# Tiles 6 and 7 transposed by DMA, weights loaded in halves and behind transposes, and a new order, in a two-block linear-attention kernel

## The chip, the cores and the metric

One Trainium2 chip, one core. The metric is device time in microseconds (us) of one execution; the profile is of one such execution and is shown in us from the start of its span. Names of engines: PE is the matrix engine (PEld its weight loads), ACT the scalar engine, DVE the vector engine, POOL the GpSimd engine, SP the engine that issues the DMAs.

## What is computed

Four layers, attention (A), dense (B), A, B, on one sequence of 2048 rows of 512 bf16 numbers; each is added to its input.

```python
x = A_x
x = x + _A_ref(_layernorm(x), A_wqkv, A_wo)
x = x + _B_ref(_layernorm(x), B_w1, B_w2)
x = x + _A_ref(_layernorm(x), A_wqkv, A_wo)
x = x + _B_ref(_layernorm(x), B_w1, B_w2)
```

A is linear attention with 32 heads of 16: q, k, v are the three 512-wide parts of `x @ wqkv`; with `phi(t) = (t + 1 if t > 0 else exp(t)) + 1e-6`, each head forms `kv = phi(k)^T v` and `z = sum phi(k)`, and the output is `(phi(q) kv) / (phi(q) z + 1e-6)` times `wo`. B is `relu(x @ w1) @ w2` with 1376 hidden columns.

## The kernel before, in words

The 2048 rows are 16 tiles of 128 rows; four tiles make a chunk (tile i is in chunk i // 4). All weights and activations stay on the chip. The kernel doesn't write its instructions down in order: each step is added to a graph with what it reads and writes (`_Graph.add`, `add_flex` for a step that either of two engines may do), and a list scheduler (`_list_schedule`) puts the steps of each engine into one fixed order, by a planner's costs (`C_...`) and a table `HINTS` that moves single steps forward or back or picks an engine (a key with "!"). So a new table moves steps everywhere. Each engine then runs its own order and waits in it for semaphores; nothing overtakes. PSUM has 8 banks of 128 x 512; a step that opens a bank waits until the one before in it was read out.

The start of the first layer, with the names that the planner uses and their lines:

- `ld_x0`, `ld_x1`, `ld_x2`, ... (L465, L471): input tiles 0, 1, 2 to 3, 4 to 7, 8 to 11, 12 to 15. `ld_wk`, `ld_wq`, `ld_wv0` (L470), `ld_wvl` (L479), `ld_wo`, `ld_w1`, `ld_w2a`, `ld_w2b` (L481 to L488): the weights. All DMAs are issued by SP, in one order, on one queue.
- `bnst`, `bnag` (L534, L535, DVE) make mean and variance of a tile. `lnv`, `rstd` make the inverse deviation: for tiles 0 to 3 and for whole chunks 2 and 3 on ACT (L540, L542), for tiles 4 to 7 as `veps` on DVE and a power on POOL (L545, L547). `norm` (L572, DVE) writes the normalized tile to `xn`.
- `trp` (L600, PE) transposes tiles 0 to 7 with four 128-wide matmuls against an identity, `trev` (L606 ACT, L607 DVE) copies the result from PSUM to `Tb`. After `trp` of tiles 0 and 1 there is a `fill` (L529), four matmuls on zeros. Tiles 8 to 15 are transposed by DMA, two tiles at a time (`tr2_0` to `tr3_1`, L586), as are all tiles in the later layers.
- `kproj` (one tile, four matmuls of 512 columns, one for each quarter of the contraction over 512), `qh` (chunk 0, half a chunk, four steps of four 256-column matmuls) and `qproj` (a chunk, four steps) are the products with wk and wq (L635, as are all matmul groups). Each result is read twice by ACT (`lin` L618, `exp` L620), then `em` (L622) and `phi` (L628) on DVE make phi of it.
- `g0_3`, `g0_0`, ... (PE) collect `phi(k)^T` times the normalized tiles; the first ones need phi of the four tiles of chunk 0. They have no read-out on ACT until all chunks are in.

At the end of the first layer `fin` (PE, one tile each) makes the output of a tile, `resid` (L642, DVE) adds it, `sq` (L650, ACT) and small steps on POOL and DVE make the statistics, `norm` (L576 DVE or POOL, L581 ACT) normalizes, and `tr0_0`, `tr0_1`, `tr1_0`, ... (L586) transpose by DMA; `tr1_1` holds tiles 6 and 7. The second layer then begins with `hr0`, `h0_0`, ..., `hr1`, where `hr1` needs the four tiles of chunk 1; `trh0` (L826) is a DMA transpose of the result of `hr0`.

Of the kernel before, what the change touches and what calls it, by code (L numbers as in the profile page):

```python
# [1385 lines left out]
```

## Time and profile before

| what | value |
|---|---|
| median of 3 runs | 268.78 us (268.74 to 269.23) |
| the profiled execution | 268.93 us, of which the span of its instructions is 267.2 us |
| PE busy, instructions | 262.0 us, 2020 matmuls recorded |
| DVE, ACT, POOL busy | 226.2, 187.0, 58.5 us |
| granted clock of PE | full in every slice |
| HBM read, written | 7.14 MB, 2.10 MB |

The page lists groups of instructions by line, engine and tiles (`out<-in`). The chain of waits follows the end of the span back from each instruction to what released it. The view of waits adds up the idle time of an engine by what ended it. The view of one tile gives, for instructions that touch it, durations, starts and, for DMAs, the time from issue to landing. The timeline merges equal instructions that follow each other ("x4"); the length of a merged row of matmuls holds the latency of its last one too, the chain's does not.

### The profile page before, as it was taken

To read this page: it belongs to the slowest core of one execution; us is meant where nothing else is said; L and a number is where in the kernel's file an instruction comes from. 1 tells how busy PE (TensorE), PEld (TensorE's weight loads), DVE (VectorE), ACT (ScalarE), POOL (GpSimd) and SP (SyncE) were. 2 spreads that over 40 slices of the span, in tenths; PEclk is the share of its full clock that TensorE was granted. 3 is DMA by queue.
4 is the path that set the end of the run, shared out by engine and by line. 5 is a ranking of instruction groups with operands and counts; after the bars stand their busy time and mean duration, and the time that the engine had idled before them with its cause. 6 is when DMAs were issued, how large, how long until landed. Compare 5 with 4: busy or idle time off the path is not lost.

```text
span 267.2 us, 5481 instructions
## 1 busy us (share of the span) xinstructions
PE 262.0 (98%) x2020; PEld 183.1 (69%) x2020; DVE 226.2 (85%) x636; ACT 187.0 (70%) x408; POOL 58.5 (22%) x146
## 2 busy tenths in 40 slices
PE   7999999999989999999999999999999999999995
PEld 3664547644745798857768755674488789888884
DVE  5799974789888999997998675459999999899994
ACT  4998896766975237999667797787899936057400
POOL 3210000026682001403103430000744434000000
PEclk9999999999999999999999999999999999999999
DMA  7986620763765000400400421054373223402003
GB/s 205 368 285 137 197 42 3 157 146 65 86 120 98 2 20 2 89 11 2 79 2 0 79 54 28 2 129 108 62 153 68 39 39 101 81 0 72 28 34 126
DMA packets 44890, 22.18 MB, mean 83 GB/s; under 512 B 34784, under 2 KB 43328, under 8 KB 44864
## 3 DMA queue, kind: packets, MB, share of 16 engines
q1 hardware_dynamic: 44864, 21.83, 34.3%
q8 instruction: 16, 0.26, 0.4%
q14 instruction: 10, 0.08, 0.1%
HBM read 7.14 MB, written 2.10 MB: 35 GB/s over the span
## 4 chain that ended last, share of the span: by engine, by line
PE 92%; ACT 3%; DMA 3%; DVE 1%; SPq 0%; issue 0%; DVEq 0%
PE ps L635 91%; ACT sqscr L650 2%; DMA Tb<-xn 2%; DMA xin<-in_A_x_dram 1%; PE ps L600 1%; ACT xn L581 1%; DVE xres L642 0%; DVE bst L534 0%; PE ps L529 0%; DVE rdc L1064 0%; SPq L471 0%; DVEq L1324 0%; DVE xn L572 0%; ACT big L946 0%
## 5 line engine op out<-in xcount | busy, mean ns | idle before, releaser
L618 ACT ACTIVATE big<-ps 128x512 bf16<-128x512 f32 x64 | 40.7, 644 | 9.5 <-PE ps L635 9.4
L650 ACT ACTIVATE sqscr<-xres 128x512 bf16<-128x512 f32 x48 | 30.0, 625 | 9.1 <-DVE xres L642 5.1
L635 PE MATMUL ps<-Tb,w 128*128 128x256 f16 (+1 forms) x216 | 35.3, 304 | 0.0
L635 PE MATMUL ps<-w,big 128*128 128x256 bf16 (+1 forms) x256 | 32.4, 272 | 0.0
L635 PE MATMUL ps<-wqkv,Tb 128*128 128x512 bf16 x128 | 31.2, 379 | 0.0
L635 PE MATMUL ps<-big,xn 128*128 128x256 bf16 (+1 forms) x224 | 31.1, 288 | 0.0
L635 PE MATMUL ps<-Tb,wqkv 128*128 128x512 f16 (+1 forms) x144 | 30.8, 355 | 0.0
L620 ACT ACTIVATE escr<-ps 128x512 bf16<-128x512 f32 x48 | 29.6, 634 | 1.1 <-PE ps L635 1.1
L635 PE MATMUL ps<-Mf,big 128*128 128x512 bf16 x128 | 29.6, 379 | 0.0
L635 PEld LDWEIGHTS ps<-w,big 128*128 128x128 bf16 (+1 forms) x256 | 24.9, 98 | 3.6 <-ACT big L946 0.3
L635 PEld LDWEIGHTS ps<-big,xn 128*128 128x128 f16 x224 | 21.3, 98 | 8.5 <-issue 0.8
L635 PEld LDWEIGHTS ps<-Tb,w 128*128 128x128 bf16 x216 | 20.6, 98 | 8.8 <-DMA Tb<-xn 0.4
L908 ACT ACTIVATE escr<-ps 128x512 f32<-128x512 f32 (+1 forms) x40 | 20.3, 544 | 8.1 <-PE ps L635 7.4
L895 DVE TENSOR_TENSOR big<-ps,escr 128x512 bf16<-128x512 f32 (+1 forms) x40 | 23.6, 603 | 1.7 <-ACT escr L908 1.1
L564 POOL TENSOR_TENSOR rstd<-veps,nhalf 128x2 f32<-128x2 f32 x24 | 20.4, 853 | 7.9 <-DVE veps L562 6.8
L635 PEld LDWEIGHTS ps<-Tb,wqkv 128*128 128x128 bf16 x144 | 13.7, 98 | 11.7 <-ACT escr L620 0.3
L635 PEld LDWEIGHTS ps<-Mf,big 128*128 128x128 bf16 x128 | 12.3, 98 | 13.8 <-ACT Mf L717 0.2
L622 DVE TENSOR_SCALAR escr<-escr 128x512 bf16<-128x512 bf16 x48 | 13.7, 289 | 8.6 <-ACT escr L620 8.4
L635 PEld LDWEIGHTS ps<-wqkv,Tb 128*128 128x128 f16 x128 | 12.2, 98 | 12.4 <-ACT Tb L606 0.4
L628 DVE TENSOR_TENSOR big<-big,escr 128x512 bf16<-128x512 bf16 x48 | 19.8, 419 | 0.8 <-ACT big L618 0.2
L581 ACT ACTIVATE xn<-xres,nbias,rstd 128x512 f16<-128x512 f32 x21 | 16.8, 815 | 5.1 <-DVE nbias L566 3.9
L898 ACT ACTIVATE big<-big 128x512 bf16<-128x512 bf16 (+1 forms) x31 | 16.2, 542 | 4.8 <-DVE big L895 4.7
(116 smaller groups left out, 515.9 us busy)
## 6 DMA issues: line engine op xcount, KB each, us to landing
big<-rdc SPq DMA_DIRECT2D x32, 128.0 KB, 2.7
wqkv<-in_A_wqkv_dram SPq DMA_DIRECT2D x3, 512.0 KB, 7.0
xin<-in_A_x_dram SPq DMA_DIRECT2D x3, 512.0 KB, 7.8
w<-in_B_w_dram SPq DMA_DIRECT2D x1, 1376.0 KB, 14.5
w<-in_B_w_dram SPq DMA_DIRECT2D x1, 1280.0 KB, 7.0
wo<-in_A_wo_dram SPq DMA_DIRECT2D x1, 512.0 KB, 10.3
out_dram<-GT SPq DMA_DIRECT2D x1, 512.0 KB, 4.1
out_dram<-Mf SPq DMA_DIRECT2D x1, 512.0 KB, 2.6
```

Of the source, the lines that this page charges most:

```text
L564: g.add(POOL, lambda e: e.tensor_tensor(rstd[:, sl], veps[:, sl], nhalf[:, 0:n], ALU.pow), [("veps", lo), ("nhalf",)], [("rstd", i) for i ...
L581: (ACT, lambda e: e.activation(xn[:, i, :], src, ACTF.Identity, scale=rstd[:, i:i + 1], bias=nbias[:, i:i + 1]), C_ACT_SB_AP)],
L600: last = e.transpose(psb()[:, 128 * c:128 * c + 128], xn[:, i, 128 * c:128 * c + 128], ident[:])
L618: g.add(ACT, lambda e: e.activation(dst_ap, psv[:, b, :], ACTF.Identity, bias=1.0 + 1e-6, scale=1.0), [("ps", b)], [dst_key], C_ACT_PSUM, ...
L620: g.add(ACT, lambda e: e.activation(sap, psv[:, b, :], ACTF.Exp), [("ps", b)], skeys, C_ACT_EXP, name=name + "_exp")
L622: g.add(DVE, lambda e: e.tensor_scalar(sap, sap, 1.0, 1e-6, ALU.min, ALU.add), skeys, skeys, C_DVE_BF4X, name=name + "_em")
L628: g.add(DVE, lambda e: e.tensor_tensor(dst_ap, dst_ap, sap, ALU.max), [dst_key] + skeys, [dst_key], 340.0, name=name + "_phi")
L635: last = e.matmul(o, l, r, start=st, stop=sp, skip_group_check=skip)
L650: g.add(ACT, lambda e: e.activation(sqscr[:, q, :], xres[:, i, :], ACTF.Square, scale=math.sqrt(INV_D), accum_out=s2[:, i:i + 1]), xr(i), ...
L895: g.add(DVE, lambda e: e.tensor_tensor(ap, sh(psv[:, bank, 0:w]), sh(other()), ALU.add), [("ps", bank)] + okeys + ([] if first else bk), q ...
L898: g.add_flex([(ACT, lambda e: e.activation(ap, ap, ACTF.Relu), C_ACT_PSUM if len(cs) == 2 else 270.0), (DVE, lambda e: e.tensor_scalar(ap, ...
L908: g.add(ACT, lambda e, w=w: e.activation(q[:, 0:w], psv[:, bank, 0:w], ACTF.Identity), [("ps", bank)], key, C_ACT_PSUM if len(cs) == 2 els ...
```

## The change

- **Tiles 6 and 7**: statistics together on ACT, and one DMA transpose (`tr1_1`) in place of two `trp`; tiles 0 to 5 stay on PE. The rule `hi - lo >= 2` sends that pair's `lnv` and `rstd` to ACT.
- **Loads**: wk and wq come in two halves of the contraction each (`wka`, `wkb`, `wqa`, `wqb`). `wv0` and `wvl` are tied behind the norms of tiles 6 and 7, `wo`, `w1` and `w2` behind those of tiles 12 to 15.
- **First use in halves**: `kproj` of tiles 0 and 1 and the `qh` steps are split by halves of the contraction.
- **Zeros**: the `fill` after tile 1 is gone.
- **First norms** of tiles 1 to 7 may go to POOL; the planner's table put none there.
- **New order**: another `HINTS` table, and other planner values for when loads land.

The order that the scheduler makes of it, at the start, by the planner's names (the first norms are called `fnorm` in the changed kernel and `norm` here; a `kproj` or `qh` with a last digit 0 or 1 is one half of the contraction):

```
SP before  ld_x0 ld_x1 ld_x2 ld_wk ld_x4 ld_wq ld_x12 ld_x8 ld_wv0 ld_wvl ld_wo ld_w1 tr2_0 tr2_1 ld_w2a ld_w2b tr3_1 tr3_0
SP after   ld_x0 ld_x1 ld_wka ld_x2 ld_wkb ld_wqa ld_x4 ld_wqb ld_x12 ld_x8 tr1_1 ld_wvl ld_wv0 tr2_0 tr2_1 tr3_1 tr3_0 ld_wo ld_w1 ld_w2a ld_w2b

PE before  trp0 fill0 trp1 fill1 kproj0 trp2 kproj1 trp3 kproj2 kproj3 qh0_0_3 qh0_1_3 qh0_0_0 qh0_0_1 trp4 ... kproj4 trp5 g0_3_0 g0_0_0
PE after   trp0 fill0 trp1 kproj0_0 kproj0_1 kproj1_0 [qh, first half of wq, x4] kproj1_1 trp2 trp3 [qh, second half, x4]
           kproj2 kproj3 [qh of tiles 2 and 3, x4] trp4 [qh x2] trp5 [qh x2] kproj4 kproj5 qproj1_1 kproj6 kproj7 qproj1_2 qproj1_3 g0_3_0 g0_0_0

DVE after  bnst0 bnag0 bnst1 norm0 bnag1 norm1 bnst2 bnst3 bnag2 bnag3 k0_em norm2 norm3 bnst6 bnst7 bnst4 bnag6 bnag7 bnag4 bnst5
           veps4 k1_em bnag5 norm6 veps5 norm7 norm4 k1_phi norm5 k2_em k3_em k2_phi bnst12 bnst14 bnag12 bnst9 bnag14 k4_em
           bnag9 bnst11 bnst8 bnag11 k0_phi bnag8 bnst10 q0_2_em bnag10 k4_phi q0_2_phi k3_phi

ACT after  lnv0 rstd0 lnv1 rstd1 trev0 trev1 lnv2 k0_exp rstd2 lnv3 rstd3 k1_lin trev2 trev3 k1_exp lnv6 k0_lin rstd6
           k2_lin k2_exp k3_lin k3_exp trev4 q0_0_lin trev5
```

At the end of the first layer `fin7` stands two `fin` steps earlier among the others (before `fin12` and `fin13`, not behind them), the norm of tile 6 is on DVE (behind `resid15`) and no longer on ACT, and on SP `tr1_1` stands ahead of `trh0`.

The core of the diff:

```diff
-        ld_w(slice(D, 2 * D), "wk")
+        ld_w(slice(D, 2 * D), "wka", slice(0, 2))
         ld_x(2, 4)
-        ld_w(slice(0, D), "wq")
+        ld_w(slice(D, 2 * D), "wkb", slice(2, 4))
+        ld_w(slice(0, D), "wqa", slice(0, 2))
+        ld_w(slice(0, D), "wqb", slice(2, 4))
...
+        def tied(load, names):
+            n = len(g.ops)
+            load()
+            for o in g.ops[n:]:
+                o.sdeps += [p for p in g.ops[:n] if p.name in names and p not in o.sdeps]
...
-            if i < 2:
+            if i < 1:
                 warm_fill(i)
...
+            parts = ((0, 1, "wka"), (2, 3, "wkb")) if first_k and i < 2 else ((0, 1, 2, 3, "wka", "wkb"),)
...
+                for k, key in enumerate(("wqa", "wqb")):
+                    mm_group(lambda b=b, j=j, k=k: [(psv[:, b, 256 * h:256 * h + 256], wqkv[:, c, 128 * j:128 * j + 128], Tb[:, i0:i0 + 2, c, :],
+                                                     h == 0 and c == 0, c == 3, True) for c in (2 * k, 2 * k + 1)],
+                             [("T", i0), ("T", i0 + 1), (key,)], [("ps", b)], 2 * C_MM256, "qh%d_%d_%d_%d" % (t, h, j, k))
...
-                if t < FIRST_PE_CHUNKS:
+                if t < FIRST_PE_CHUNKS and i < 6:
...
+            if t == 1:
+                ln_part_first(6, 8)
+                ln_norm(6, True)
+                ln_norm(7, True)
+                tr_dma(1, 1)
...
+            if t == 1:
+                tied(loads_a, ["fnorm6", "fnorm7"])
...
+                        if t + 3 == NCH - 1:
+                            tied(loads_b, ["fnorm%d" % i for i in range(NT - 4, NT)])
```

More of the change, by code (lines that the diff above doesn't have):

```diff
@@ L465, in ld_x, with ld_w @@
             dma(lambda e: e.dma_start(xin[:, lo:hi, :], x_v[:, lo - 1:hi - 1, :]), [], [("xin", i) for i in range(lo, hi)],
-                350.0 * (hi - lo), "ld_x%d" % lo, issue=C_LOAD_ISSUE, late={1: 100.0, 2: 200.0}.get(lo, C_LATE))
+                350.0 * (hi - lo), "ld_x%d" % lo, issue=C_LOAD_ISSUE, late={1: 100.0, 2: 650.0}.get(lo, C_LATE))
         wq_v = A_wqkv.rearrange("(c p) n -> p c n", p=128)
-        def ld_w(sl, key):
-            dma(lambda e: e.dma_start(wqkv[:, :, sl], wq_v[:, :, sl]), [], [(key,)], 1480.0, "ld_" + key, issue=C_LOAD_ISSUE, late=500.0 if key == "wk" else C_LATE)
+        def ld_w(sl, key, cs=slice(0, 4)):
+            dma(lambda e: e.dma_start(wqkv[:, cs, sl], wq_v[:, cs, sl]), [], [(key,)], 370.0 * (cs.stop - cs.start), "ld_" + key,
+                issue=C_LOAD_ISSUE, late=700.0 if key[:2] == "wk" else C_LATE)
@@ L471, in build_kernel @@
         dma(lambda e: e.dma_start(xin[:, 0, :], x_h), [], [("xin", 0)], 370.0, "ld_x0", issue=C_LOAD_ISSUE, late=-350.0)
         ld_x(1, 2)
-        ld_w(slice(D, 2 * D), "wk")
+        ld_w(slice(D, 2 * D), "wka", slice(0, 2))
         ld_x(2, 4)
-        ld_w(slice(0, D), "wq")
+        ld_w(slice(D, 2 * D), "wkb", slice(2, 4))
+        ld_w(slice(0, D), "wqa", slice(0, 2))
+        ld_w(slice(0, D), "wqb", slice(2, 4))
         for t in range(1, NCH):
             ld_x(4 * t, 4 * t + 4)
-        ld_w(slice(2 * D, 3 * D), "wv0")
@@ L487, in build_kernel, with loads_a @@
-        if FLAST < 128:
-            dma(lambda e: e.dma_start(w2[0:FLAST, NFC - 1, :], B_w2[nfull * 128:DFF, :]), [], [("w2b",)], 600.0, "ld_w2b", issue=C_LOAD_ISSUE)
+        def tied(load, names):
[3 more added lines that the diff above has]
+                o.sdeps += [p for p in g.ops[:n] if p.name in names and p not in o.sdeps]
+        def loads_a():
+            ld_w(slice(2 * D, 3 * D), "wv0")
+            dma(lambda e: e.dma_start(wvl[:], A_wqkv[D - 1:D, 2 * D:3 * D].broadcast_to([128, D])), [], [("wvl",)], 2000.0, "ld_wvl",
+                issue=C_LOAD_ISSUE)
@@ new lines, in loads_b @@
+        def loads_b():
+            dma(lambda e: e.dma_start(wo[:], A_wo.rearrange("(c p) n -> p c n", p=128)), [], [("wo",)], 1500.0, "ld_wo", issue=C_LOAD_ISSUE)
+            dma(lambda e: e.dma_start(w1[:], B_w1.rearrange("(c p) n -> p c n", p=128)), [], [("w1",)], 4500.0, "ld_w1", issue=C_LOAD_ISSUE)
+            dma(lambda e: e.dma_start(w2[:, 0:nfull, :], B_w2[0:nfull * 128, :].rearrange("(c p) n -> p c n", p=128)),
+                [], [("w2a",)], 5500.0, "ld_w2a", issue=C_LOAD_ISSUE)
+            if FLAST < 128:
+                dma(lambda e: e.dma_start(w2[0:FLAST, NFC - 1, :], B_w2[nfull * 128:DFF, :]), [], [("w2b",)], 600.0, "ld_w2b", issue=C_LOAD_ISSUE)
@@ L489, in build_kernel @@
         W2KEYS = [("w2a",), ("w2b",)] if FLAST < 128 else [("w2a",)]
-        ALL_LOADS = [("wk",), ("wq",)]
+        ALL_LOADS = [("wka",), ("wkb",), ("wqa",), ("wqb",)]
         def _table(e):
@@ L571, in ln_norm @@
             if first:
-                g.add(DVE, lambda e: e.tensor_scalar(xn[:, i, :], xin[:, i, :], mv[:, i, 0:1], rstd[:, i:i + 1], ALU.subtract, ALU.mult),
-                      [("xin", i), ("mean", i), ("rstd", i)], [("xn", i)], C_DVE_NORM_BF, name="norm%d" % i)
+                f = (lambda e: e.tensor_scalar(xn[:, i, :], xin[:, i, :], mv[:, i, 0:1], rstd[:, i:i + 1], ALU.subtract, ALU.mult))
+                g.add_flex([(DVE, f, C_DVE_NORM_BF)] + ([(POOL, f, C_POOL_NORM)] if 0 < i < 8 else []),
+                           [("xin", i), ("mean", i), ("rstd", i)], [("xn", i)], name="fnorm%d" % i)
                 return
@@ L651, in sq, with a_k @@
                   xr(i), [("sqscr", q), ("s2", i)], C_ACT_SQ, name="sq%d" % i)
-        def a_k(i):
+        def a_k(i, first_k=False):
             b = alloc_bank()
-            mm_group(lambda: [(psv[:, b, :], Tb[:, i, c, :], wqkv[:, c, D:2 * D], c == 0, c == 3, False) for c in range(4)],
-                     [("T", i), ("wk",)], [("ps", b)], 4 * C_MM512, "kproj%d" % i)
+            parts = ((0, 1, "wka"), (2, 3, "wkb")) if first_k and i < 2 else ((0, 1, 2, 3, "wka", "wkb"),)
+            for k, p in enumerate(parts):
+                cs = [c for c in p if isinstance(c, int)]
+                mm_group(lambda cs=cs: [(psv[:, b, :], Tb[:, i, c, :], wqkv[:, c, D:2 * D], c == 0, c == 3, False) for c in cs],
+                         [("T", i)] + [(c,) for c in p if not isinstance(c, int)], [("ps", b)], len(cs) * C_MM512,
+                         "kproj%d" % i if len(parts) == 1 else "kproj%d_%d" % (i, k))
             phi_evac(b, pk_tile(i), ("big", pk_unit(i)), "k%d" % i, stt=(i % 4) < K_STT)
@@ L729, in a_q @@
                                             c == 0, c == 3, False) for c in range(4)],
-                         [("T", i) for i in range(4 * t, 4 * t + 4)] + [("wq",)], [("ps", b)], 4 * C_MM512, "qproj%d_%d" % (t, j))
+                         [("T", i) for i in range(4 * t, 4 * t + 4)] + [("wqa",), ("wqb",)], [("ps", b)], 4 * C_MM512, "qproj%d_%d" % (t, j))
                 q_evac(t, j, b, first)
@@ L740, in a_q_half @@
                 i0 = 4 * t + 2 * h
-                mm_group(lambda b=b, j=j: [(psv[:, b, 256 * h:256 * h + 256], wqkv[:, c, 128 * j:128 * j + 128], Tb[:, i0:i0 + 2, c, :],
-                                            h == 0 and c == 0, c == 3, True) for c in range(4)],
-                         [("T", i0), ("T", i0 + 1), ("wq",)], [("ps", b)], 4 * C_MM256, "qh%d_%d_%d" % (t, h, j))
+                for k, key in enumerate(("wqa", "wqb")):
+                    mm_group(lambda b=b, j=j, k=k: [(psv[:, b, 256 * h:256 * h + 256], wqkv[:, c, 128 * j:128 * j + 128], Tb[:, i0:i0 + 2, c, :],
+                                                     h == 0 and c == 0, c == 3, True) for c in (2 * k, 2 * k + 1)],
+                             [("T", i0), ("T", i0 + 1), (key,)], [("ps", b)], 2 * C_MM256, "qh%d_%d_%d_%d" % (t, h, j, k))
                 if h == 1:
```

12 lines of the change are left out of this document (3 added, 9 removed), and 124 rows, old and new, of the table HINTS.

## Prediction

> **What bounds the kernel now.** I read the page first, its busy times and its chain of what ended last:
>
> ```profile
> PE 262.0 (98%) x2020; PEld 183.1 (69%) x2020; DVE 226.2 (85%) x636; ACT 187.0 (70%) x408; POOL 58.5 (22%) x146
> ...
> PE 92%; ACT 3%; DMA 3%; DVE 1%; SPq 0%; issue 0%; DVEq 0%
> ```
>
> PE works nearly all the time and the chain is PE's: PE sets the end. So an edit is worth what it takes from PE's work, from PE's start or from PE's idle time; all else is cover. Next, PE's own waits. Behind the zeros at the start there is one:
>
> ```profile
> PE ps L635 <- DMA Tb<-xn: 0.8, 1, 0.8
> ```
>
> Third, the chain in order of time (start, us, what):
>
> ```profile
> 6.00 0.56 PE ps L600 x4
> 6.57 0.22 PE ps L529 x4
> 6.79 0.98 PE ps L635 x4
> ...
> 18.37 0.22 PE ps L600 x4
> 18.59 0.87 PE ps L635 x8
> 19.46 0.22 PE ps L600 x4
> 19.69 43.25 PE ps L635 x264
> ...
> 71.85 4.67 DMA Tb<-xn
> 76.51 0.05 issue
> 76.56 187.63 PE ps L635 x1544
> ```
>
> From 6.79 PE is dense; a PE transpose (L600) in the stream costs 0.22 us; at 76.5 PE waits 0.83 for a DMA transpose issued at 71.85 (tiles 6 and 7 of the second layer, ahead of `hr1`); behind it no wait to the end at 264.2. So the whole room is small: 0.22 a transpose, tenths at the start, 0.83.
>
> Last, the landings. The view of the tile wqkv, cut to the issue of wk and then to that of wq, gives
>
> ```profile
> L470 SPq DMA_DIRECT2D wqkv<-in_A_wqkv_dram x1: 434/434/434, 2.2 to 2.2; - x1
> ...
> DMA to landing us min/median/max: 4.5/4.5/4.5
> ```
> ```profile
> L470 SPq DMA_DIRECT2D wqkv<-in_A_wqkv_dram x1: 443/443/443, 3.2 to 3.2; - x1
> ...
> DMA to landing us min/median/max: 7.0/7.0/7.0
> ```
>
> wk lands at 2.2 + 4.5 = 6.7, wq at 3.2 + 7.0 = 10.2. The same view of xin gives tile 0 at 0.8 + 2.1 = 2.9, tile 1 at 1.2 + 2.6 = 3.9, tiles 2 and 3 at 1.7 + 3.1 = 4.8, tiles 4 to 7 at 2.7 + 6.0 = 8.7. Between landings, 256 KB (tiles 2, 3) took 0.9 and 512 KB (wk) 1.9. kproj0 at 6.79 thus followed both wk (6.7) and the end of the zeros (6.57 + 0.22).
>
> **The change, part by part.**
>
> *Two PE transposes gone.* 2 x 0.22 = **-0.44** on PE's stream. Their copies out of PSUM (0.42 each, DVE L607) go too; `veps` and the power on POOL become lnv6 and rstd6 on ACT. That matters only through DVE and ACT below.
>
> *First product earlier.* Without the second zeros PE is free at 6.57. wka stands third in the queue, where 256 KB landed at 4.8; tile 0 is copied out at 5.61 + 0.60 = 6.2. So kproj0 begins at 6.57 and not 6.79: **-0.22**. Its second half needs wkb at 7.0; 1 MB is through by then as before (wk, 6.7). Two bounds: 0 (if the halves come 0.3 late) and -0.3 (PE could not begin before tile 0 is there).
>
> *Second half of wq.* After kproj0 (0.87: four matmuls, by the row 18.59) PE does half of kproj1 (to 7.87; tile 1 is out at 7.2), four half steps of qh (0.87, to 8.74; wqa by about 7.6, a quarter of the way from 6.7 to 10.2), the rest of kproj1 (9.17) and trp2, trp3 (9.61). Then it wants wqb. Ahead of wqb stand the same 2 MB as ahead of the end of wq before, so I take 10.2: PE waits **+0.6**. Nothing hides this: PE's order is fixed, and kproj2 behind it waits too. Bounds: 0 (landing by 9.6) and +1.6 (11.2, under the rivals). Before, PE came to wq only at 10.8, behind kproj2 and kproj3, so this wait is new.
>
> *DVE in front of g0_3.* trp2 and trp3 want norm2 and norm3: k0_exp on ACT starts 0.22 behind kproj0 (6.79 to 7.81 before, less four matmuls), at 7.66, rstd2 0.48 later, rstd3 at 8.5; the norms run at 8.5 and 8.9 and end by 9.3, just in time. Tiles 4 to 7 land at about 9.3 (10.2 less 0.9 for wqb). From 9.3 to the end of k3_phi DVE has, by starts in the timeline, 10 bn_stats of 0.61, 10 bn_aggr of 0.09, 4 norms of 0.32, 5 em of 0.25 (0.21 to 0.29), 6 phi of 0.35 and 2 small ones: 11.6. k3_phi ends at about 21.0. PE, from 10.2, has four half steps of qh (0.9), the eight of tiles 2 and 3 (1.7), kproj2 to 7 (5.2), trp4 and trp5 (0.4) and three qproj (2.6): 10.8, so it comes to g0_3_0 at 21.0. I take **+0.1** (0 to +0.5): before, k3_phi was done by 14.2 and had no part in this.
>
> *Tiles 6 and 7 by DMA.* norm7 ends on DVE about 4.0 after 9.3 (4 bn_stats, 4 bn_aggr, one em, two norms and small ones), so tr1_1 is issued at 13.3, behind nothing on SP that waits longer; tiles 8 to 11, the last load ahead in the queue, land at 4.4 + 8.4 = 12.8. Its own time is 3.0 (the first two of the second layer: 3.0, 3.0) to 5.1 (the one issued at 69.1): landing at 16.3 to 18.4. PE wants it for qproj1_1 at 16.7. I take 3.0, since the queue is empty then as at 62.1, and the wait at **0**. Behind the waiting tr1_1 on SP stand wvl and wv0, not used before 24 (L661).
>
> *Weights behind transposes.* wv0 leaves at about 15, wo to w2 (3.3 MB) with tiles 12 to 15 at about 34. wo is used at 50.2, w1 at 66.2, w2 at 75.5 (L965). At 1 MB in 3.5 us they are in by about 46. Cost 0; the first to feel a delay are the spreads of 1/den, issued from 45.3 on the same queue.
>
> *Order at the end of layer 1.* The 0.83 us stand behind this: norm of tile 6 on ACT, 70.87 + 0.80, then trh0's issue (70.56 + 1.19), then 4.7 of DMA. In the new order fin7 stands two steps (2 x 0.87) earlier, the norm is on DVE behind resid15 (which ended at 70.0), and trh0 stands behind. tr1_1 can leave at about 70.5; even at 4.7 it lands at 75.2, PE comes at 75.7. I take **-0.83**; bounds 0 and -0.83. Elsewhere the order changes too, but PE was dense there: nothing to win, so 0, with what can be lost under the rivals. The stretch behind 264.2 keeps its steps.
>
> Sum: -0.44 - 0.22 + 0.6 + 0.1 - 0.83 = **-0.79**. The profiled execution (268.93, span 267.2) goes to 268.1; it stands 0.15 above the median, so I forecast 268.78 - 0.79 = **268.0 us**.
>
> **The rivals.**
>
> - *No waits at the start*: wqb by 9.6 and k3_phi early. For it: less stands behind the loads. Against: those bytes stood behind before too. -0.44 - 0.22 - 0.83 = -1.49: 267.3.
> - *The wait ahead of hr1 comes back.* For it: those transposes took 5.1 and 4.7, and in 71.5 to 73.9 us the view of the DMAs has a load of code in the same engines:
>
> ```profile
> q8 instruction: 1, 0.02, 4.0%
> ```
>
>   If that hits the earlier tr1_1 harder, or norm6 slips on DVE, only -0.44 + 0.48 = +0.04 is left: 268.8.
> - *Tiles 6 and 7 land late* (the other side). Place: qproj1_1. At 5.1 they land at 18.4 and PE waits 1.7, of which the 0.1 at g0_3 is taken back: -0.79 + 1.6 = +0.8, 269.6. It decides from a landing at about 17.6 on. Against: nothing else is in the queue. The Trainium skill, "VectorE: DVE Perf Modes", Rules for kernel authors, speaks for this rival: transpose 128 x 128 on TensorE where PSUM will do, by DMA only otherwise. By that rule tiles 6 and 7 belonged on PE; the trace agrees on the latency (3.0 against 0.22), not on which of the two is on PE's path.
> - *The halves come slower than wholes.* Tile 1's 128 KB took 1.0 between landings, as much as the 256 KB behind; if each of the two more DMAs costs such a half us, wqb lands at 11.2 and PE loses 0.9 more: +0.1, 268.9. Against: 256 KB in 0.9 and 512 KB in 1.9 are one rate. The Trainium skill, "DMA: Bandwidth & Descriptors", Bandwidth, says to batch DMAs to 1 MiB or more; from its table (64 KB 0.95 us, 1 MB 6.15 us) I estimate 0.7 a split, wqb at 11.6 and 269.3. The 0.9 and 1.9 here don't agree with it.
> - *New waits behind 77 us.* The new order is tight in other places; each wait like the 0.83 costs as much, two of them give +0.87: 269.7. Against: the planner's order of before has one such wait in 260 us.
> - That the change does nothing is out: the built order has 24 PE transposes for 32 and 29 DMA transposes for 28.
>
> **Chances.** Forecast 0.38, no waits at the start 0.18, wait ahead of hr1 0.16, tiles 6 and 7 late 0.10, slow halves 0.06, new waits 0.12. About 0.2% (0.54 us) is what a measurement can tell from no change: below 268.24 counts as faster. Of the forecast's 0.38, 0.26 lies there and 0.12 within (its start terms at their upper bounds): faster 0.26 + 0.18 = 0.44, same 0.12 + 0.16 + 0.06 = 0.34, slower 0.10 + 0.12 = 0.22. The range goes from 267.2 (no waits at the start, PE at tile 0's landing) to 269.6 (tiles 6 and 7 late) and leaves out the new waits and what lies beyond.
>
> **What would show it.** Right: 24 L600 matmuls; the first L635 at 6.5 to 6.6; one PE wait of about 0.6 ending near 10.2, put down to the wqkv load; none at 76. The forecast is wrong if PE has waits behind 22 us, or if the wait for wqb is under 0.2 or over 1.2.

## The result and the profile after

| | before | after |
|---|---|---|
| median of 7 runs each | 268.74 us (268.12 to 269.23) | 270.05 us (269.54 to 271.05) |
| ratio | | 1.0057, 95% interval 1.0035 to 1.0079 |
| the profiled execution, its span | 268.93, 267.2 | 269.73, 267.9 |

The change costs 1.3 us in the median, 0.8 between the two profiled executions; the forecast was 0.8 less. The page of the changed kernel (its lines are some 25 further down in the code, PE's products are L660):

```profile
PE 261.8 (98%) x2008; PEld 182.5 (68%) x2008; DVE 225.7 (84%) x621; ACT 186.5 (70%) x413; POOL 59.5 (22%) x152
...
PE 86%; ACT 6%; DMA 3%; DVE 1%; SPq 1%; issue 1%; POOL 1%; DVEq 0%
```

PE has 12 matmuls fewer and is still the chain, but only for 86% of it instead of 92. PE's waits (us in total, times, longest) name the rest:

```profile
PE ps L660 <- DMA Tb<-xn: 1.1, 1, 1.1
PE ps L660 <- DMA wqkv<-in_A_wqkv_dram: 0.5, 1, 0.5
PE ps L660 <- DVE big L653: 0.2, 1, 0.2
```

and the chain in order of time (start, us, what) says where they are:

```profile
4.19 5.82 DMA wqkv<-in_A_wqkv_dram
10.05 3.65 PE ps L660 x24
...
14.59 149.52 PE ps L660 x1072
...
168.61 0.44 DVE big L653
169.09 14.42 PE ps L660 x112
...
199.24 3.25 DMA Tb<-xn
202.63 62.31 PE ps L660 x580
```

wqb lands at 10.01 and lets PE go on at 10.05, as forecast. The wait at 76 us is gone, as forecast. But at 169 PE waits for phi of tile 13 (`k13_phi`; 0.2 by the view, 0.4 by the records of the matmuls), and at 202.6 for a DMA transpose of tiles 6 and 7, issued at 199.24, this time that of the last layer: a wait that the kernel before does not have.

To see how much each place costs, I took from the records of the matmuls when each kernel has the same PE work left. The table gives that time less the profiled execution of before, at points of before's clock (the experiments' rows are used further down):

| us later than before at | 13 | 57 | 78 | 163 | 188 | 200 | 206 | end |
|---|---|---|---|---|---|---|---|---|
| after | -0.33 | 0.07 | -0.93 | -1.04 | -0.41 | -0.64 | 0.72 | 0.74 |
| g0, after again | 0.56 | 0.96 | -0.04 | -0.16 | 0.47 | 0.24 | 1.63 | 1.65 |
| f1 | 0.16 | 0.67 | -0.33 | -0.45 | 0.17 | 0.15 | 1.76 | 1.78 |
| g1 | 0.44 | 0.88 | -0.12 | -0.24 | 0.39 | 0.17 | 0.93 | 0.95 |
| h1 | 0.30 | 0.87 | -0.13 | -0.26 | 0.37 | 0.77 | 0.77 | 0.79 |
| k1 | 0.04 | 0.51 | -0.49 | -0.62 | -0.03 | -0.25 | 0.34 | 0.36 |
| h3 | -0.32 | 0.46 | -0.54 | -0.67 | -0.45 | 0.62 | 0.62 | 0.64 |
| k2 | -0.33 | 0.45 | -0.55 | -0.67 | -0.45 | -0.06 | -0.06 | -0.04 |
| g5 | 1.11 | 1.51 | 0.51 | 0.37 | 0.37 | 0.95 | 1.25 | 1.31 |
| f4 | 0.31 | 0.31 | 0.23 | 0.12 | 0.12 | 0.07 | 1.00 | 1.07 |
| g6 | -0.24 | -0.24 | -0.23 | 0.64 | 1.27 | 1.04 | 1.66 | 1.67 |
| e6 | 0.41 | 0.63 | 0.66 | 0.55 | 4.80 | 4.80 | 4.80 | 4.81 |
| s1 | 2.45 | 2.45 | 1.84 | 1.80 | 1.80 | 1.76 | 1.76 | 1.80 |

Read the first row by its steps: the start -0.33; to 57 us +0.40 (mostly the `den` steps, below); the wait ahead of `hr1` of the second layer -1.00; to 163 -0.11; the second attention +0.63 (0.4 ahead of `g0_3_3`, 0.2 for a `den`); to 200 -0.23; then +1.36 within 4 us, the wait at 202.6 (1.25 by the starts of PE's products; the view's 1.1 leaves out the latency of the last one) and 0.11 behind it; sum +0.72. The first profile of the changed kernel was also a good one: in g0 it starts 0.9 later, and ends 0.9 later too, so what the start wins or loses is still there at the end. (One execution in the experiments, h2's profiled one, ran at a granted clock of 0.755; it is left out of the ratio, and its trace is not read.)

`den` is a planner's name for four matmuls on 32 columns of the array that make the sums for the divisions. In both profiles a `den` by itself costs 0.2 us more than one that stands next to another; before, five of the eight stood in groups, after only two.

### The profile page after: what moved, and what is told of

Read it like the earlier page. It is cut to its first block, busy times and chain, and to the rows that moved or that the text cites. A ratio compares the mean times of both kernels' runs of the same rounds, so it can differ in the third digit from the quotient of the medians.

```text
span 267.9 us, 5464 instructions
## 1 busy us (share of the span) xinstructions
PE 261.8 (98%) x2008; PEld 182.5 (68%) x2008; DVE 225.7 (84%) x621; ACT 186.5 (70%) x413; POOL 59.5 (22%) x152
## 4 chain that ended last, share of the span: by engine, by line
PE 86%; ACT 6%; DMA 3%; DVE 1%; SPq 1%; issue 1%; POOL 1%; DVEq 0%
PE ps L660 86%; DMA wqkv<-in_A_wqkv_dram 2%; ACT sqscr L675 2%; DMA Tb<-xn 1%; ACT escr L938 1%; DVE xres L667 1%; ACT big L643 1%; ACT escr L645 1%; ACT xn L606 1%; SPq L477 1%; SPq L482 0%; POOL rstd L588 0%; ACT lnd L783 0%; PE ps L625 0%; DVE big L653 0%
## 5 line engine op out<-in xcount | busy, mean ns | idle before, releaser
L643 ACT ACTIVATE big<-ps 128x512 bf16<-128x512 f32 x64 | 39.0, 639 | 10.5 <-PE ps L660 10.5
L660 PE MATMUL ps<-Tb,w 128*128 128x256 f16 (+1 forms) x216 | 36.1, 304 | 0.0
L660 PE MATMUL ps<-w,big 128*128 128x256 bf16 (+1 forms) x256 | 32.3, 272 | 0.0
L660 PE MATMUL ps<-Tb,wqkv 128*128 128x512 f16 (+1 forms) x144 | 31.5, 356 | 0.5 <-DMA wqkv<-in_A_wqkv_dram 0.5
L660 PE MATMUL ps<-big,xn 128*128 128x256 bf16 (+1 forms) x224 | 31.6, 288 | 0.2 <-DVE big L653 0.2
L660 PE MATMUL ps<-wqkv,Tb 128*128 128x512 bf16 x128 | 30.6, 379 | 0.0
L660 PE MATMUL ps<-Mf,big 128*128 128x512 bf16 x128 | 29.4, 379 | 0.0
L660 PEld LDWEIGHTS ps<-big,xn 128*128 128x128 f16 x224 | 21.2, 98 | 9.5 <-issue 0.9
L660 PEld LDWEIGHTS ps<-w,big 128*128 128x128 bf16 (+1 forms) x256 | 24.9, 98 | 3.7 <-ACT big L976 0.3
L660 PEld LDWEIGHTS ps<-Tb,w 128*128 128x128 bf16 x216 | 20.8, 98 | 8.8 <-DMA Tb<-xn 0.2
L660 PEld LDWEIGHTS ps<-Tb,wqkv 128*128 128x128 bf16 x144 | 13.5, 98 | 12.7 <-DMA wqkv<-in_A_wqkv_dram 1.0
L660 PEld LDWEIGHTS ps<-Mf,big 128*128 128x128 bf16 x128 | 12.3, 98 | 13.8 <-DVE Mf L747 0.2
L580 POOL TENSOR_SCALAR mean<-s 128x2 f32<-128x2 f32 x24 | 7.2, 299 | 62.1 <-DVE xres L667 59.6
L660 PEld LDWEIGHTS ps<-wqkv,Tb 128*128 128x128 f16 x128 | 12.5, 99 | 12.4 <-ACT Tb L631 0.5
L588 POOL TENSOR_TENSOR rstd<-veps,nhalf 128x2 f32<-128x2 f32 x24 | 18.8, 784 | 7.1 <-DVE veps L586 6.4
L606 ACT ACTIVATE xn<-xres,nbias,rstd 128x512 f16<-128x512 f32 x19 | 15.2, 810 | 6.6 <-POOL nbias L590 3.4
```

Source lines behind the costliest of these rows:

```text
L580: g.add(POOL, lambda e: e.tensor_scalar(mean[:, sl], s1[:, sl], -INV_D, None, ALU.mult), [("s1", i) for i in tl], [("mean", i) for i in tl ...
L588: g.add(POOL, lambda e: e.tensor_tensor(rstd[:, sl], veps[:, sl], nhalf[:, 0:n], ALU.pow), [("veps", lo), ("nhalf",)], [("rstd", i) for i ...
L606: (ACT, lambda e: e.activation(xn[:, i, :], src, ACTF.Identity, scale=rstd[:, i:i + 1], bias=nbias[:, i:i + 1]), C_ACT_SB_AP)],
L643: g.add(ACT, lambda e: e.activation(dst_ap, psv[:, b, :], ACTF.Identity, bias=1.0 + 1e-6, scale=1.0), [("ps", b)], [dst_key], C_ACT_PSUM, ...
L660: last = e.matmul(o, l, r, start=st, stop=sp, skip_group_check=skip)
```

## The experiments

Each was run beside the kernel before on the same chip, in five batches on five chips (e; f; g; h with s; k). Ratios are to the kernel before of the same batch, with the 95% interval; across batches compare these and not the medians.

| run | median us | ratio |
|---|---|---|
| g0 after again | 270.28 | 1.0064 (1.0039 to 1.0089) |
| e1 | 270.70 | 1.0059 (1.0033 to 1.0085) |
| f1 | 271.29 | 1.0086 (1.0057 to 1.0114) |
| f2 | 271.01 | 1.0078 (1.0049 to 1.0107) |
| f3 | 272.40 | 1.0115 (1.0074 to 1.0156) |
| g1 | 269.82 | 1.0046 (1.0021 to 1.0070) |
| h1 | 269.78 | 1.0033 (1.0010 to 1.0056) |
| h2 | 270.01 | 1.0031 (1.0007 to 1.0055) |
| h3 | 269.26 | 1.0016 (0.9996 to 1.0035) |
| k1 | 269.75 | 1.0044 (1.0019 to 1.0069) |
| k2 | 269.11 | 0.9999 (0.9976 to 1.0022) |
| f4, before with one SP step moved | 269.81 | 1.0031 (1.0006 to 1.0056) |
| s1, before with quarter loads | 270.25 | 1.0042 (1.0017 to 1.0066) |
| e6, before with two den moved | 273.48 | 1.0154 (1.0105 to 1.0203) |
| g5, start after, rest before | 269.28 | 1.0019 (0.9997 to 1.0041) |
| g6, start before, rest after | 270.78 | 1.0072 (1.0047 to 1.0096) |
| e7, e8, mixed hints | 271.53, 291.12 | 1.0092, 1.0798 |

In the orders below a leading digit is the layer, from 0, under which the planner files a step (`2.tr1_1`: made by the second attention, wanted by `3.hr1_0`); lines with + and - are steps moved in the order of one engine.

### First theory: one wait ahead of hr1 (e1, f1, g1)

Theory A: the wait at 202.6 is what the change lost. SP's order in the changed kernel has two issues, `3.trh0` and the spread of 1/den, ahead of the transpose that PE waits for.

```diff
 SP: 2.tr1_0,
+    2.tr1_1,
     3.trh0, 2.spread3_1,
-    2.tr1_1,
     2.spread3_0
```

e1 and f1 have this edit; in e1 the planner also gave out the PSUM banks anew, in f1 everything else is the changed kernel's.

> The changed kernel, with one step moved on SP alone: the DMA transpose of tiles 6 and 7 of the last layer goes ahead of trh0 and of the spread of 1/den that stand in front of it; every other step of every engine keeps its place. Theory A (the new order costs the time: above all the 1.1 us that PE waits at 201.4 for that transpose, issued 199.24, landed 202.49): its inputs are there at 197.0, so it is issued at 197.3, lands by 200.6, PE does not wait, and the time falls by 1.1 to 1.25 us, from 270.05 to about 268.9. Theory B (the edits at the start and the loads cost it, and the wait only shows time that would be lost in any case): the time stays within 0.3 of 270.05.

> The changed kernel again with the DMA transpose of tiles 6 and 7 of the last layer ahead of trh0 and of the spread on SP, and this time with nothing else moved: in the first run of this move (e1) the planner had also given the PSUM banks out anew. Theory A (the wait of 1.25 us ahead of hr1 is what the change lost): -1.1 to -1.25, to about 268.9. Theory C (a wait behind the wait: PE, come 1.2 us earlier, runs into the evictions on ACT that it had been ahead of by nothing, as e1's waits of 0.95 and 0.41 ahead of h5_1_0 and h6_1_0 hint): hr1_0 starts without a wait, but half or more comes back within the next 5 us: 269.4 to 270.1.

Theory A fell. In both `hr1_0` starts without a wait, and nothing is won: between 200 and 206 us f1 loses 1.61 where after lost 1.36. f1's PE waits, the first line:

```profile
PE ps L695 <- DVE big L960: 1.4, 1, 1.4
```

and DVE's timeline behind it (start, us, ..., in brackets idle time before it and what ended it):

```profile
202.89 0.58 DVE L836 TENSOR_TENSOR big<-big 128x512 bf16<-128x512 bf16 x1 [1.59 <-DMA big<-rdc]
```

The spread that was overtaken now lands at 202.87, DVE stands in `pqs3_1` waiting for it, and the read-out that PE needs is queued behind that. g1 serves both: f1, and on DVE

```diff
 DVE: 3.hc22_0_2,
-     2.pqs3_1,
      3.hc22r_0_2, 3.hs1_1, 3.hc11_1_0, 3.hs2_1,
+     2.pqs3_1,
      2.pqs3_0
```

> The changed kernel with the transpose of tiles 6 and 7 of the last layer ahead of trh0 and of the spread on SP, as in f1, and in addition one step moved on DVE: pqs3_1, which waits for that spread, goes four steps back, next to pqs3_0. In f1 DVE waited 1.6 us in pqs3_1 for the spread that now came later, and PE behind it 1.4 for an eviction. Theory A2 (two transfers in a row on SP, each with an early consumer: one wanted by PE, one by DVE; both consumers must be served): no wait ahead of hr1_0 and none ahead of h5_1_0, -1.2 to -1.4 against the changed kernel. Theory C2 (yet another wait follows): less than half of it.

> The changed kernel as it is, once more, beside the other three, as their reference. Expected: about 270 us; and, since in e1 and f1, whose starts are the same, the profiled execution was 0.5 to 0.6 us later at 13 us than in the first profile of the changed kernel, a spread of some 2 us over its executions.

Between 200 and 206 us g1 loses 0.76 where g0 loses 1.39; its median is 0.46 lower. Half: DVE still waits 0.4 for a spread. The reason is seen on SP: five issues stand in a row there from 195 us on, and each of them has a consumer that is early.

### One part of the order alone, in the kernel before (f4)

```diff
 SP: 2.tr1_0, 2.spread3_0, 3.trh0,
+    2.spread3_1,
     2.tr1_1,
-    2.spread3_1,
```

> The kernel before with one part of the new order alone: on SP the spread of 1/den (spread3_1) ahead of the transpose of tiles 6 and 7 of the last layer, as in the changed kernel. Its issue then goes from 198.61 to about 199.25 and its landing from 201.84 to 202.5, while hr1_0 started at 202.02. Theory A: PE waits 0.4 to 0.5 there: 269.2 to 269.5 against the 268.7 to 269.0 of before. Theory B (late order does not matter, the start does): no change.

PE now waits there in the kernel before too (0.6 of the 1.3; the 0.8 is the known one at 76 us), and the time goes up by 0.8 us (ratio 1.0031):

```profile
PE ps L670 <- DMA Tb<-xn: 1.3, 2, 0.8
```

More than I had put: `tr1_1` left at 199.39 and not 199.25. So an issue of 0.6 us on SP at this place is an issue of 0.6 us and more on PE.

### Where the parts meet: start and rest swapped (g5, g6, and e7, e8)

e7 and e8 exchanged the hints of the later layers between the two kernels.

> The changed kernel with all its edits, but with the planner's hints of the kernel before for the steps of layers 2 to 4; from the second layer on the order of the steps on PE, POOL and SP is then that of the kernel before. Theory A: the start's gain (-0.33 behind 12 us) less the split den steps of the first layer (+0.2 to +0.4) stays, the 1.1 at 202 us goes; the wait of 0.83 at 76 us may come back or not: 267.9 to 268.8. Theory B: the start is the same, so the time is that of the changed kernel, 269.7 to 270.4.

> The other half: the kernel before, none of the edits, but with the changed kernel's hints for the steps of layers 2 to 4; SP's order behind the first layer is then the changed kernel's, PE's nearly. Theory A: the waits of that order come into the kernel before: about 1.1 ahead of hr1 of the last layer, 0.4 in the second attention, 0.2 for its split den steps, with the 0.83 at 76 us kept or gone: 269.6 to 270.4. Theory B: 268.7 to 269.0, as before.

They tell nothing clean: with half a table exchanged, the planner put the other layers in another order as well (e7 waits 1.2 us at 18 and 0.8 at 20 us, where neither kernel does; e8 up to 5.3 us at a time). So I wrote the orders out: g5 is the changed kernel to the first step of the second layer, about 65 us, and has the kernel before's order on each engine behind that; g6 the other way round.

> The changed kernel's edits and its order up to the second layer's first step (some 65 us), and behind that the kernel before's order on every engine, step by step. By the traces: the start (-0.33 at 13 us), the split den steps of the first layer (+0.34), and the wait of 0.83 to 1.0 ahead of hr1 of the second layer back: within 0.3 of the kernel before, 268.5 to 269.1. Theory B (the edits at the start cost the time): 269.8 to 270.4.

> The counterpart: none of the edits, the kernel before up to the second layer's first step, and behind that the changed kernel's order on every engine. By the traces: -1.0 (the wait ahead of hr1 of the second layer gone) +0.4 (g0_3_3) +0.1 (den2 apart) +1.36 (hr1 of the last layer and what follows): +0.6 to +0.9, 269.4 to 269.7. Theory B: 268.0 to 268.8, no slower than before.

The late order alone costs 1.9 us (g6), the early part alone 0.5 with an interval that holds zero (g5); both came out above what I had put, g6 by 1.1 us, of which 0.9 is a wait near 155 us that is explained below. Theory B, that the start costs the 1.3, is out. But both expectations were wrong in one thing that turned out to be the key. g5 has the kernel before's order around `hr1` of the second layer and does not wait there (from 57 to 78 us it wins 1.00). g6 has the changed kernel's order there and waits 0.8, as the kernel before does. So that wait does not hang on the order of the steps.

### What it hangs on: the load of code

Each trace has, on a queue of its own (q8), 16 transfers of 16 KB, kind "instruction", one for about every 256 of PE's instructions (a matmul is two, its weight load and itself). Set beside the transposes of tiles 6 and 7 and their neighbours:

| run, place | load of code at | transpose issued at, landed after, issue took |
|---|---|---|
| before, hr1 of layer 2 | 71.7 | 69.1: 5.1, 1.23; 71.85: 4.7, 2.55; PE waits 0.8 |
| g6 | 74.3 | 71.2: 5.1, 1.23; PE waits 0.8 |
| after | 75.9 | 69.9: 3.4, 1.23; 71.6: 3.3, 1.23; no wait |
| g5 | 77.9 | 70.8: 3.2, 1.23; 73.5: 3.1, 1.27; no wait |
| before, last layer | 194.3 | tr1_0 195.4: 3.1, 1.23 |
| after | 195.8 | tr1_0 195.2: 3.4, 1.97 |
| g0 | 196.5 | tr1_0 196.1: 3.2, 1.86 |
| h1 | 197.2 | tr1_0 196.0: 4.1, 1.28 |
| g5 | 197.9 | tr1_0 195.8: 4.8, 1.23 |
| h3 | 195.8 | tr1_0 195.2: 4.8, 2.85 |
| k1 | 194.1 | tr1_0 195.6: 3.2, 1.23 |

To see whether this holds beyond the places picked, I took every transpose of two tiles in the 19 traces (h2's is left out). With no load of code under way between issue and landing (455 of them), none held SP for more than 1.37 us, 446 landed after 3.0 to 3.4 and nine after 3.5 to 4.0. Of the 90 with one, 33 were as quick; the other 57 landed after up to 5.2 us or held SP for up to 2.85. So a load of code can stretch a transpose, and does not always. SP's timeline (start, us, line, operation, tiles) at 195 us, first the kernel before, then the changed one:

```profile
195.38 1.23 SPq L586 DMA_TRANSPOSE Tb<-xn  x1
196.66 0.59 SPq L765 DMA_DIRECT2D big<-rdc  x1
197.29 1.28 SPq L826 DMA_TRANSPOSE big<-hr  x1
198.61 1.31 SPq L586 DMA_TRANSPOSE Tb<-xn  x1
```
```profile
195.22 1.97 SPq L611 DMA_TRANSPOSE Tb<-xn  x1
197.24 1.27 SPq L856 DMA_TRANSPOSE big<-hr  x1
198.55 0.59 SPq L795 DMA_DIRECT2D big<-rdc  x1
199.24 1.31 SPq L611 DMA_TRANSPOSE Tb<-xn  x1
```

The same two issues stand between the two transposes, in another order. That tr1_1 leaves 0.63 later comes from the 0.74 by which the first issue is longer (it began 0.16 earlier). g6 has one more such meeting: a load at 152.7 in the transposes issued at 149.8 and 151.1 (landed after 4.9 and 4.5), for which PE waits 0.8; in the kernel before it comes at 154.2, they land after 3.2 and 3.1, and nobody waits. The view of the DMAs shows the load in the window 195.2 to 196.8 of after, and in 194.0 to 195.4 of before, just ahead:

```profile
q8 instruction: 1, 0.02, 3.5%
issues: line engine op xcount, KB each, median us to landing
Tb<-xn SPq DMA_TRANSPOSE x1, 3.4
```
```profile
q8 instruction: 1, 0.02, 4.6%
issues: line engine op xcount, KB each, median us to landing
big<-rdc SPq DMA_DIRECT2D x1, 128.0 KB, 3.3
Tb<-xn SPq DMA_TRANSPOSE x1, 3.1
```

The change moved it by taking PE work away: 12 matmuls fewer are 24 PE instructions fewer, so a load comes some 12 matmuls further on in PE's order. Counted by the matmuls left when it comes, from before to after, this is 12 for the middle one of the 16 loads, but 26 for the one at 76 us and 29 for the one at 196; between before and g6, which have equally many, single loads differ by up to 14. So the count tells the place only roughly. "Runtime: NRT & Kernel Launch", Instruction fetch mechanics, in the Trainium skill, says that an engine's code is refilled in blocks of 16 KiB, 256 instructions, by a DMA of the engine's own queue, at a cost that is mostly hidden. The traces agree on the size and on the spacing (16 loads for some 4050 PE instructions in after). They differ on hidden: PE does not wait for its code, but transposes beside it do, by 0.7 to 2 us in the rows above.

### Taking the collision away (h1, h2, h3, k1, k2)

First another try at SP's order. h1 issues the two spreads, whose inputs are ready at 192.1, while SP waits for the inputs of tr1_0:

```diff
 SP: 2.spread3_3,
+    2.spread3_1, 2.spread3_0,
     2.tr1_0,
+    2.tr1_1,
     3.trh0,
-    2.spread3_1, 2.tr1_1, 2.spread3_0
```

h2 also puts `2.g1_0_1` ahead of `2.g0_3_3` on PE; h3 is h2 with whole loads of wk and wq (`ld_w(slice(D, 2 * D), "wka", "wkb")` and the same for wq, one DMA each, at the place of the first half).

> The changed kernel with three steps moved on SP and none elsewhere: the spreads spread3_1 and spread3_0 go ahead of the transpose tr1_0 of the last layer (their inputs are ready at 192.1, and SP stood idle from 193.8 to 195.2 waiting for tr1_0's), and the transpose of tiles 6 and 7 ahead of trh0. Theory A3 (SP's queue order alone holds the loss at 199 to 204 us): hr1_0 and the evictions behind it come without a wait, -1.3 to -1.4 against the changed kernel (270.28 in its last run): 268.9. Theory C3 (DVE or ACT limit PE there in any order): a loss of 0.5 or more stays, 269.5 to 270.2.

> As h1, and on PE g1_0_1 of the second attention ahead of g0_3_3, whose wait of 0.4 for k13_phi it covers. A3: 0.4 below h1, about 268.5, a little below the kernel before. C3: 269.1 to 269.8.

> As h2, with wk and wq loaded whole again (the place of each in SP's order that of its first half; two transfers fewer; the first product then waits for all of wk, the first half steps of qh for all of wq), the order on all other engines kept. If each transfer costs some 0.35 us of its own: wk lands by 5.8, wq by 8.2, tiles 4 to 7 by 9.6, 0.5 earlier than in the median execution of the changed kernel: 0.3 to 0.8 below h2, 267.7 to 268.2. If only bytes count: tiles 4 to 7 land as before, and it is h2's time within 0.2.

In h1 neither `hr1_0` nor DVE waits any more, but now `h1_1_0` does, for tr1_0: 0.61 lost in h1, 1.28 in h3, where the load of code holds its issue for 2.85 us (table above). SP's order alone was not it. h1's median lies in the range of C3, but not for C3's reason: what limits PE there is a landing, and not DVE or ACT. h2's median is not below h1's. h3, which has the same cover of `g0_3_3`, shows that the cover works: from 163 to 188 us its row loses 0.22, where h1's loses 0.63. At 188 us PE is 0.82 earlier in h3 than in h1, and tr1_0 leaves 0.82 earlier (195.19, 196.01). But it lands at 199.96 and 200.11, because h3's load of code holds it up longer.

Then the collision itself. k1 and k2 issue the 16 products of 512 columns in `kproj12` to `kproj15` of the second attention as two of 256 each: the same PE time (0.22 as 2 x 0.11), 32 PE instructions more, so that the loads of code behind 166 us come some 16 matmuls earlier in PE's order.

```diff
-                mm_group(lambda cs=cs: [(psv[:, b, :], Tb[:, i, c, :], wqkv[:, c, D:2 * D], c == 0, c == 3, False) for c in cs],
+                halves = ((0, 512),) if first_k or i < 12 else ((0, 256), (256, 512))
+                mm_group(lambda cs=cs: [(psv[:, b, lo:hi], Tb[:, i, c, :], wqkv[:, c, D + lo:D + hi], c == 0 and lo == 0, c == 3, len(halves) > 1)
+                                        for c in cs for lo, hi in halves],
```

k1 is this edit in the changed kernel and nothing else, k2 is h3 with it.

> The changed kernel with one thing changed: the 16 products of 512 columns in the steps kproj12 to 15 of the second attention (163 to 166.5 us) are issued as 32 of 256 columns (0.22 a product as 2 x 0.11), so that 32 more PE instructions stand ahead of 195 us and the load of code comes some 1.7 us earlier, at about 194, ahead of tr1_0. Theory F (the load of code met tr1_0): tr1_0's issue takes 1.2 instead of 1.9, tr1_1 leaves 0.7 earlier, PE's wait ahead of hr1_0 falls from 1.25 to about 0.5: 269.4 to 269.7 against 270.28 of the changed kernel's last run. Theory A (the order on SP alone): no change, 270.0 to 270.5.

> h3 (whole loads, spreads early, transpose of tiles 6 and 7 ahead of trh0, g1_0_1 ahead of g0_3_3) with the same 16 products split. Theory F: the wait of 1.28 ahead of h1_1_0 goes, 1.0 to 1.3 below h3 (269.26): 268.0 to 268.3, and below the kernel before. Theory A: as h3, 269.1 to 269.4.

The traces bear theory F out. In k1 the load comes at 194.1, and SP's timeline is the changed kernel's order with the short issue:

```profile
195.61 1.23 SPq L646 DMA_TRANSPOSE Tb<-xn  x1
196.88 1.28 SPq L893 DMA_TRANSPOSE big<-hr  x1
198.21 0.59 SPq L832 DMA_DIRECT2D big<-rdc  x1
198.90 1.33 SPq L646 DMA_TRANSPOSE Tb<-xn  x1
```

PE's wait ahead of `hr1_0` is 0.49 instead of 1.25 (1.14 in g0), the loss from 200 to 206 is 0.59 instead of 1.39. From tr1_0's issue to tr1_1's landing it takes 7.27 and 7.17 us in after and g0, 6.51 in k1 and 6.46 in the kernel before. k1's time is 0.5 below g0's by the ratios, but their intervals overlap, so the traces carry this verdict. k2 is level with the kernel before (0.9999), and its interval lies below that of the changed kernel in g0. It does not beat the kernel before, though, and 268.0 to 268.3 was expected: its load of code, at 193.7, held up the issue of a spread instead (1.5 us from 193.76 to the next one at 195.24, which is 0.65 elsewhere), and PE still waited for tr1_0 (first line; 0.6 with what it takes to start again).

```profile
PE ps L757 <- DMA Tb<-xn: 0.4, 1, 0.4
PE ps L757 <- DMA wqkv<-in_A_wqkv_dram: 0.3, 1, 0.3
```

### The start (f2, s1, h3)

wq's second half landed at 10.0, 10.3, 10.5, 10.6, 10.6, 10.8, 10.9, 10.9 and 11.4 us in nine traces with the changed kernel's loads, whole wq at 9.8, 9.9, 10.0, 10.2 and 10.3 in the five with the kernel before's, behind the same 2 MB. s1 splits in the kernel before:

```diff
-            dma(lambda e: e.dma_start(wqkv[:, :, sl], wq_v[:, :, sl]), [], [(key,)], ...)
+            for c in range(4):
+                dma(lambda e, c=c: e.dma_start(wqkv[:, c:c + 1, sl], wq_v[:, c:c + 1, sl]), [], [(key + str(c),)], ...)
```

> The kernel before with nothing changed but its two loads wk and wq, each issued as four of 128 KB (one chunk of the contraction each), every consumer waiting for all four as before. If each of the six more transfers costs 0.35 us: wq is there at 12.1 instead of 10.0, and PE, which wants it at 10.8, waits 1.3: about 270. If only bytes count: wq at 9.8 to 10.3, and no change, 268.7 to 268.9.

The last quarter of wk landed at 7.7 (whole: 6.3 to 6.9), the last of wq at 11.7 (whole: 10.0 by the median of the five). Six more transfers, 1.7 us: 0.28 each. (The time went up by 1.5 us, but not by this alone: behind the wait of 1.2 for wk the granted clock was 0.50 until 10.9.) At about 0.3 us for each transfer beside its bytes, two more make 10.0 to 10.6, where the median of the halves' landings is. But this is one execution of s1, and the order counts as well: with wq ahead of tiles 4 to 7, the same 2 MB were in at 9.5 and 9.4 in six transfers (h3, k2), at 9.4 in eight (f2) and at 10.7 in eight (f3). So a price of 0.3 a transfer is not shown; that the halves land later than the whole in the order of the two kernels, and scatter more, is. The Trainium skill's table ("DMA: Bandwidth & Descriptors", Bandwidth), from which I had estimated 0.7 a split, gives more than twice s1's figure.

f2 moved wqb ahead of the load of tiles 4 to 7:

```diff
 SP: ld_wqa,
+    ld_wqb,
     ld_x4,
-    ld_wqb,
```

> The changed kernel with one step moved on SP: the load of wq's second half goes ahead of the load of tiles 4 to 7. wqb then lands at about 8.5 instead of 10.0, ahead of where PE wants it (9.4), and tiles 4 to 7 land 0.7 later, at about 10.0. If PE's wait for wqb is lost time: -0.5, 269.5. If DVE behind tiles 4 to 7 is the bound up to k3_phi (ended at 20.6, g0_3_0 starts at 20.9), that end moves to 21.3 and PE waits there instead: 0 to +0.4, 270.0 to 270.4.

wqb landed at 8.1 and PE did not wait for it, but 0.45 at the transpose of tile 4, whose norm came later; by 17 us PE stood where the first profile of after had it (-0.29 against -0.33). The wait moved. The whole loads of h3 and k2 gave -0.3 at 13 us and -0.05 at 17, twice; the halves -0.3 to 1.1 at 13. By the ratios h3 is 0.4 us below h2, with overlapping intervals.

### The den steps, and all at once (e6, f3)

e6: in the kernel before, `0.den2` behind four steps `g1_2_2` to `g0_2_3`, and `2.den2` ahead of `2.qproj3_0`. f3: f1, f2, `2.g1_0_1` ahead of `2.g0_3_3`, and `0.den0` next to `0.den2`.

> The kernel before, with two of its adjacent den steps (four products of 32 rows each) pulled apart: den2 of the first layer four steps later, den2 of the second attention some eight steps later; nothing else moves. Theory A counts 0.2 us for every den that stands alone among products of 128 rows (0.09 ahead of it, 0.11 behind it, in both traces): two more such places, +0.4, 269.1. Rival: the 0.2 belongs to what a den is beside, or is hidden: 268.7, no change.

> The changed kernel with both SP moves (tiles 6 and 7 of the last layer first; wqb ahead of tiles 4 to 7) and two PE moves: g1_0_1 of the second attention ahead of g0_3_3 to cover its wait of 0.4, and den0 of the first layer next to den2 (0.12 less by the traces). Theory A: -1.2 -0.5 -0.4 -0.1 from 270.05: about 267.9, below both kernels. Theory C, with the waits shifting: 268.8 to 269.6.

In e6 the first split costs what was expected, 0.22 (0.41 at 13 us, 0.63 at 57). The second cannot be read: moved, it made PE wait 2.3 us for a read-out on DVE, and the time went to 273.5. f3, at 272.40, missed the ranges of both theories. It shows the same of `den0`: PE waits 1.0 behind it for a read-out on ACT. It also waits 1.3 at the transpose of tile 4, as f2 does for 0.45, and loses the 1.9 from 200 to 206 that f1's edit brings. Its cover of `g0_3_3` holds: no wait is left there. In these orders hardly a step can be moved by itself.

## Why the prediction was wrong

- *Two PE transposes gone, first product earlier, second half of wq, DVE in front of g0_3.* These terms sum to +0.04. Measured at 13 us: -0.33 in the first profile, and -0.33 to 1.11 with a mean of 0.3 in the eight traces with this start, against a mean of 0.2 in the five traces with the kernel before's. Right in the sum. The wait for wqb was forecast at 0.6 and is up to 1.8 from run to run (0.5 in the first profile; where it is under 0.2, in f1, h1 and k1, PE had waited 0.4 to 1.1 for wqa), because PE now comes to wq ahead of a landing that scatters by 1.4 us; before it came half a us or more behind one. There was no wait ahead of `g0_3_0`. The rival of slow halves comes nearer to the landings: the median of the halves is 0.6 later than that of the wholes, where it had 1.0. Whether that is a price of each transfer stays open.
- *Tiles 6 and 7 by DMA.* Forecast to land at 16.3: 16.23. *Weights behind transposes*, in by 46: 45.9. Both at no cost, as forecast.
- *Order at the end of layer 1*, -0.83: measured -1.00, for another reason. I had tr1_1 leave 1.3 us earlier by the new order. It left 0.2 earlier (71.62), and landed after 3.3 us instead of 4.7 because the load of code had moved on to 75.9; g5 and g6 show that the order of the steps does not decide it. So the number was right by luck. I had seen that load, and put it down to chance in a rival; its place follows, roughly, from the count of PE's instructions.
- **The step that failed** is the sentence behind it: "Elsewhere the order changes too, but PE was dense there: nothing to win, so 0". Measured: +0.40 and +0.63 for split `den` steps and a wait for phi, and +1.36 at 200 us, with 0.34 won in small waits. In all +2.05 where I had put 0. Of the +1.36, 0.7 to 0.8 is the load of code, as k1 shows (0.59 against 1.39 in g0). The remaining 0.6 is mostly that tr1_0 leaves late for where PE is: at 200 us PE is 0.64 earlier than before in after, 0.24 later in g0 and 0.25 earlier in k1, and tr1_0 leaves 0.16 earlier, 0.72 later and 0.23 later (195.38 before; 195.22, 196.10, 195.61), 0.48 behind PE each time. So this chain follows PE; in the new order it is 0.48 longer. The traces point to one step. ACT's norm of tile 4, the last thing tr1_0 waits for, stands behind a read-out of the last layer in the new order (after; start, us):

```profile
193.65 0.15 DVE L590 TENSOR_TENSOR nbias<-mean,rstd 128x2 f32<-128x2 f32 x1
193.92 0.58 ACT L938 ACTIVATE escr<-ps 128x512 f32<-128x512 f32 x1
194.40 0.80 ACT L606 ACTIVATE xn<-xres,nbias,rstd 128x512 f16<-128x512 f32 x1
```

In the kernel before the norm in that place starts at 194.55, 0.08 behind the end of its `nbias`, and the read-out comes behind it. The read-out takes 0.48 of ACT's order (193.92 to 194.40). No run moved it, so this last step is argued and not shown.

- The rival of *new waits behind 77 us*, 269.7, is what the profiled execution did (269.73); it got 0.12 of the chances, on the ground that the order before had one such wait. The ground was wrong: that wait hung on where a load of code fell, and the change shifted those loads. The range ended at 269.6 and left it out.

Open: why the changed kernel scatters by 1.5 to 2.3 us over its 7 and 12 executions, and the kernel before by 2.8 to 4.0 over 19 to 35, was not taken apart beyond the landings at the start; and a version that lets the code load pass between all of SP's issues at 193 to 199 us was not found.

## What to carry to other kernels

In a kernel where PE is dense, look at what PE is fed by in each stretch: the slack there is tenths, and a new order can use it up even where PE had no wait, so "dense, nothing to win" is no reason to put its cost at nothing. Follow each chain that feeds PE (norm, DMA issue, transpose) through the new order of every engine in it. Taking out matmuls moves later loads of PE's code against the DMAs; in the profile, set the times of that queue beside the transposes before putting a price on a new order, and count PE's instructions for a rough idea of where the loads go. Take a wait out only with the next consumer in view: most mends here moved it.

## What was not expected of the hardware

- A load of 16 KB of code on q8, every 256 PE instructions or so, can stretch a DMA transpose of two tiles from 3.0 to 3.4 us to as much as 5.2, and SP's issue of it from 1.23 to as much as 2.85 (57 of the 90 transposes that met one).
- Four matmuls on 32 columns cost 0.2 us more where they stand alone between full ones (e6: 0.22). "TensorEngine Tiling (Array Packing)", Key Properties, in the Trainium skill, says that a change of the tiling mode drains TensorE; the traces fit this: they show the price of a change and the change back, not the drain itself.
- The same 2 MB at the start landed at 9.8 to 10.3 us in five traces with whole loads and at 10.0 to 11.4 in nine with halves; with both loads in quarters (s1, one trace) at 11.7.
- In e6, in the 2.4 us behind PE's wait of 2.3, the granted clock was 0.51 and products of 512 columns took 0.43 us instead of 0.22; in s1 it was 0.50 for 3.2 us behind a wait of 1.2 at the start. Behind the waits of 0.8 and 1.1 ahead of `hr1` in the two kernels it was 1.0.
